# Decay scans whose constant operand lies in PSUM, with a new written-out order, in a fused RWKV and low-rank-mixing kernel

## The chip, the cores and the metric

One NeuronCore of one Trainium2 chip runs the whole kernel in one launch. The metric is the device time of one execution in microseconds (us); lower is better. Before the change it is 448.16 us, the median of 3 runs (447.41 to 448.6).

## What is computed

Two layers follow each other. The first is a linear attention with a decay per channel: batch 4, 8 heads, 768 time steps, 48 channels per head, all in float32.

```python
for t in range(S):
    cur = np.einsum('bhd,bhe->bhde', u[None] * kt, vt)
    y[:, :, t] = np.einsum('bhd,bhde->bhe', rt, state + cur)
    state = wt[:, :, :, None] * state + np.einsum('bhd,bhe->bhde', kt, vt)
```

Its output, with the heads side by side as 384 channels, is x for the second layer: a mix over time of rank 32 (U, V) and an FFN with a hidden width of 1536.

```python
h = x.transpose(0, 2, 1) @ U @ V
u = x + h.transpose(0, 2, 1)
return u + np.maximum(u @ w_ch1, 0.0) @ w_ch2
```

## The kernel before, in words

**The attention** is cut into 24 chunks (4 batches of 6) of 128 time steps; `chunk(g)` (L347) makes the steps of one. The channels of two heads lie on the 128 partitions, four such pairs side by side in the free dimension. The decay w of a chunk comes as four segments of SEG = 129 columns, one zero and then 128 decays, and one column more at the end (L34, L359, L1166). Two scans on VectorE run along these columns, `state = w * state + constant`. Step F (`scan_f`, L385) goes from the end to the start; its constant is `resets`, with a 1 at each segment's border (L187 to L189), so it gives the product of all decays from a time to the chunk's end. Step R (L423) writes the reciprocals of the four totals to the segment starts of `qd` (L218), and step Q (`scan_q`, L398) scans forward with `qd` as its constant. Both constants lie in SBUF. RP (L404) multiplies r by Q, KS (L409) multiplies k by F; either may be on VectorE or on GpSimd. AM (L531) makes the scores on TensorE, CP (L552) masks them, YA and YZ (L615, L640) make the output, DS (L559) the state's increment in the PSUM tile `dS` (L234), and ZA and ZM (L591, L595) add it to the state and let it decay. GpSimd, VectorE or ScalarE have the small products PR, RK, RU, the diagonals SEL and SEL2 and the totals T.

**Turns through TensorE.** For the first 12 chunks, k (KT, L516) and the output (XT, L735) are transposed on TensorE, and for the first 6 the bonus rows (MD, L488) come from there. Each takes the one bank `tr`, which is free again when a copy has taken the result out (KN, XN on ScalarE, DV). Later chunks are transposed in 32 by 32 blocks on VectorE (KD, XD).

**The FFN** works on seven blocks of 384 or 512 times (L29). Mix and block: GA, SELM, HP on TensorE, UADD, UH, UL, then 12 steps UP (L859) and 12 steps DN (L893) of nine matmuls each, in float32r with weights split into a high and a low part. ScalarE or VectorE (HH) and VectorE (HL) take each UP out of its bank. The weights are converted on the chip first (E, C2, C3, ADD, HI, SUB, L287 to L342). The three `ffn` banks serve GA, SELM, HP, UP and DN.

**PSUM** has eight banks: two for the scores, one each for `tr`, `y` and `dS`, three for `ffn`.

**The order** of all 1422 steps is written out by hand in ORDER (L65): of every three characters two give the step's number in base 64, the third says whether it takes its other engine (odd), and how many dummy matmuls `lead` (L202) puts ahead of it (half of it, rounded down). `plan` (L134) only hands out buffer slots along that order. Each engine works off its own steps strictly in it.

```python
        if how % 2:
            s.eng = s.alt
        s.lead = how // 2
```

Of the kernel before, what the change touches and what calls it, by code (L numbers as in the profile page):

```python
# [33 lines left out]
SEG = P + 1  # L34
# [17 lines left out]
def channel_order():  # L52
# [18 lines left out]
    "4p04q17d04f01B00o04a00f07y00b08904b07z05614r11C04V04c00c07h04v04s04W04t04z05D04X10B10d10p05901D00q05E05F10g0"
    "8Z15G17e07-01E04w00s01F05408+00h00z05H00i04x01W04+05I08A14-07l00r14y18107f050M5J61G07g17a07c15101H10t08O05K0"
    "8508-15L00u05O08Q05M00+00j05N00-00v05P07m10k18201I07o05Q05R21008307n15S07q05T05U41107p09i07r05Y08405c07s0120"
    "5V05W05Z07u05a08E05d05e01d05X15b15f18R07v00w08001J01K07w08B17x00x01315m05p00y16208a11L07t15n08C01Y05q05o08T0"
    "5r01f07+01M01P01r08S11N08W11e01g05v01X08D09011Z08b06301a05s01Q06408F01h01b01O11R01y05t01i08r05j01S01c18J01k0"
# [25 lines left out]
    "J10J51Fx0J60J70J80J90Fy0Fz0L20F+0JJ0J21Lx0Lk0J30JD0JV0JE1JF0M40JK0Ln0JL0JW1L50JX0JY0JG0L70JZ0JA0Ja0LC0JB0JH1"
    "JI0JP0JC0JS0JM0JT0L30JQ1JU0Jv1Jb0JN0Jc0JO0JR0L60J-0Lr0Jd0Je0Jz1Lm0J+0Jh0F-0Ji0Jj0M60K00Jf0K11Jk0K20Jn0Lt0Jw1"
    "Lo0Jl0LW0K60M50L+0Jo0L00Lq0Jp0LY0Ly0Lu0K71KC0K80Jq0Lw0L40Jr0KU0KV0KX0Lp0M00KD1Js0M10KW0LX0KI0KE0KY1KJ0KZ0K30"
    "KK0Ka0KR0Jm0Kb1Kc0KL0L-0KS0KM0K41KT0M30K50KO0K90KA0KN0KP1Fv0KB0KF0Kd0L10KG0Lv0KH0Ls0Ke0KQ0M20Kf0Kg0Lz0MA0Kj0"
    "MB0Kh0Kk0Kl0MC0Km0Kp0Ki0Fp0Kn0MD0Kq0Jg0Ko0Kr0Ks0Kt0Ku0"
# [53 lines left out]
def rwkv_moe_kernel(ctx, tc, wT, rkT, vN, vS, rkN, uB, uT, uD, U, V, w1, w2, out):  # L159
# [4 lines left out]
    psT = pool("psT", 1, space=PSUM)  # L164
# [182 lines left out]
    def chunk(g):  # L347
# [133 lines left out]
        if by_pe:  # L481
            btd = Buf("tr")
# [5 lines left out]
            def rows_by_u():  # L488
                tr = st["trd"] = place("tr", [P, NP, P], f"trd_{g}", btd)
# [26 lines left out]
        def turn_k():  # L516
            tr = st["trk"] = place("tr", [P, NP, P], f"trk_{g}", btr)
# [51 lines left out]
        if on:  # L569
# [653 lines left out]
```

## Time and profile before

| What | Value |
|---|---|
| median of 3 runs | 448.16 us (447.41 to 448.6) |
| the profiled execution's own time | 448.02 us |
| its span, first to last instruction | 446.3 us |
| TensorE busy | 426.4 us, 96% |
| VectorE busy | 362.7 us, 81% |
| ScalarE busy | 189.7 us, 42% |
| GpSimd busy | 104.0 us, 23% |
| mean granted TensorE clock | 0.98 |

The profile names the engines PE (TensorE), PEld (its weight loads), DVE (VectorE), ACT (ScalarE), POOL (GpSimd) and SP (the queue that issues DMAs). A line such as "L400 DVE TENSOR_TENSOR_SCAN Q<-w,qd" is an instruction of line 400 on VectorE that writes Q from w and qd. Busy time of an engine is the union of its instructions; an instruction's duration reaches some hundredths of a microsecond into the next one.

### The profile page before, as it was taken

Reading aid. Unit: us, or ns where it says so; the run is one execution under the profiler, and the core shown is the slowest. Engines: PE = TensorE matmul, PEld = TensorE weight load, DVE = VectorE, ACT = ScalarE, POOL = GpSimd, SP = SyncE. Lnnn points to the kernel's source line nnn. Section 1 sums busy time; section 2 is a strip of 40 time slices with the busy share of each in tenths; the row PEclk is TensorE's granted clock in tenths of the full one; section 3 lists DMA queues with packets and bytes.
Section 4 is the critical chain, followed back from the end, with each engine's and each line's share of the span. In section 5 each row is a group of like instructions: output and inputs, shape, how many; then the busy total and the mean of one; then the engine's idle time right before and its main releaser. Section 6 shows DMA issues by size and latency. Waiting matters only on the chain.

```text
span 446.3 us, 9868 instructions
## 1 busy us (share of the span) xinstructions
PE 426.4 (96%) x3906; PEld 366.1 (82%) x3906; DVE 362.7 (81%) x750; ACT 189.7 (42%) x533; POOL 104.0 (23%) x123
## 2 busy tenths in 40 slices
PE   6996999999999999999999999999999999999993
PEld 4785759999999898788868788887767889999993
DVE  8999999999899999999999999999995116524610
ACT  5697988776476332565023323013634002112300
POOL 1112232432257555332225101420000100100000
PEclk9996799999999999999999999999999999999998
DMA  8966836244654635331307030174212130133020
GB/s 298 337 232 225 271 124 220 87 153 151 223 171 164 220 106 181 107 115 37 107 32 241 3 93 0 46 225 164 74 66 77 36 122 21 59 127 110 1 78 24
DMA packets 23911, 57.22 MB, mean 128 GB/s; under 512 B 2864, under 2 KB 7856, under 8 KB 23856
## 3 DMA queue, kind: packets, MB, share of 16 engines
q1 hardware_dynamic: 23856, 56.50, 38.0%
q8 instruction: 32, 0.52, 0.5%
q14 instruction: 23, 0.19, 0.1%
HBM read 51.77 MB, written 4.72 MB: 127 GB/s over the span
## 4 chain that ended last, share of the span: by engine, by line
PE 40%; DVE 16%; issue 1%; ACT 1%; DVEq 0%
PE f L899 20%; PE f L865 16%; DVE xn L720 5%; DVE kn L685 2%; DVE hid L876 2%; DVE xn L718 1%; DVE A L555 1%; DVE F L387 1%; PE aps L542 1%; DVE Q L400 1%; PE hp L816 1%; DVE xT L917 1%; PE y L622 1%; DVE Z L593 0%; PE y L632 0%
## 5 line engine op out<-in xcount | busy, mean ns | idle before, releaser
L865 PE MATMUL f<-u,w1h 128*128 128x384 f32 (+1 forms) x504 | 147.9, 364 | 1.0 <-DVE hid L876 1.0
L899 PE MATMUL f<-hid,w2h 128*128 128x384 f32 (+1 forms) x504 | 148.3, 364 | 0.0
L865 PEld LDWEIGHTS f<-u,w1h 128*128 128x128 f32 x504 | 92.9, 188 | 12.6 <-DVE hid L876 2.5
L899 PEld LDWEIGHTS f<-hid,w2h 128*128 128x128 f32 x504 | 92.9, 188 | 10.0 <-issue 1.3
L865 PE MATMUL f<-u,w1l 128*128 128x384 f32 (+1 forms) x252 | 90.7, 360 | 0.0
L899 PE MATMUL f<-hid,w2l 128*128 128x384 f32 (+1 forms) x252 | 90.7, 360 | 0.0
L870 ACT ACTIVATE hid<-f 128x384 fp32r<-128x384 f32 (+1 forms) x65 | 34.6, 538 | 106.6 <-PE f L865 104.0
L876 DVE SCALAR_TENSOR_TENSOR hid<-f,hid 128x384 fp32r<-128x384 f32 (+1 forms) x84 | 50.2, 606 | 13.4 <-ACT hid L870 12.5
L454 ACT ACTIVATE A<-ident,dv 128x128 f32<-128x128 f32 x148 | 46.6, 391 | 11.7 <-DVE dv L440 3.9
L899 PEld LDWEIGHTS f<-hid,w2l 128*128 128x128 f32 x252 | 47.4, 188 | 4.7
L865 PEld LDWEIGHTS f<-u,w1l 128*128 128x128 f32 x252 | 47.4, 188 | 4.1
L685 DVE STREAM_TRANSPOSE kn<-rk 32x128 f32<-32x128 f32 x160 | 48.3, 302 | 2.4
L917 DVE TENSOR_TENSOR xT<-f,xT 128x384 f32<-128x384 f32 (+1 forms) x21 | 12.8, 613 | 37.6 <-PE f L899 37.2
L322 POOL TENSOR_TENSOR cva_w<-cva_w,raw_w 128x384 int32<-128x384 int32 x24 | 26.2, 1100 | 70.1 <-DVE cva_w L315 51.9
L832 POOL TENSOR_TENSOR u<-xT,u 128x512 fp32r<-128x512 f32 (+1 forms) x11 | 13.5, 1236 | 92.0 <-DVE u L828 85.1
L387 DVE TENSOR_TENSOR_SCAN F<-w,resets 128x517 f32<-128x517 f32 x24 | 30.6, 1275 | 0.4 <-DMA w<-in_wT 0.2
L720 DVE STREAM_TRANSPOSE xn<-xT 32x192 f32<-32x192 f32 x80 | 29.6, 370 | 1.3 <-ACT xT L666 0.2
L400 DVE TENSOR_TENSOR_SCAN Q<-w,qd 128x516 f32<-128x516 f32 x24 | 29.3, 1223 | 0.1
L407 POOL TENSOR_TENSOR rk<-rk,Q 128x512 f32<-128x512 f32 x12 | 16.4, 1365 | 45.0 <-DVE Q L400 42.3
L461 POOL TENSOR_SCALAR_AFFINE_SELECT A<-dv 128x128 f32<-128x128 f32 (+1 forms) x33 | 11.5, 382 | 58.1 <-PE f L865 23.3
L602 ACT ACTIVATE Z<-Z,tots 128x96 f32<-128x96 f32 x60 | 17.5, 364 | 10.3 <-DVE Z L593 10.2
L1088 ACT ACTIVATE junk<-raw_w 128x384 uint8<-128x384 f32 x24 | 13.1, 544 | 19.7 <-DMA raw_w<-in_w 19.5
(123 smaller groups left out, 570.8 us busy)
## 6 DMA issues: line engine op xcount, KB each, us to landing
raw_w<-in_w SPq DMA_DIRECT2D x48, 384.0 KB, 3.9
rk<-in_rkT SPq DMA_DIRECT2D x24, 512.0 KB, 4.3
kr<-in_rkN SPq DMA_DIRECT2D x18, 384.0 KB, 4.5
w<-in_wT SPq DMA_DIRECT2D x24, 258.5 KB, 2.8
v<-in_vS SPq DMA_DIRECT2D x24, 224.0 KB, 3.9
out_dram<-xT SPq DMA_DIRECT2D x12, 192.0 KB, 2.6
out_dram<-xT SPq DMA_DIRECT2D x9, 256.0 KB, 2.5
raw_V<-in_V SPq DMA_DIRECT2D x8, 96.0 KB, 3.4
```

The lines of the kernel that those rows point to most:

```text
L322: lambda: nc.gpsimd.tensor_tensor(out=d["to"].bitcast(I32), in0=d["a"].bitcast(I32), in1=d["e"], op=ALU.add),
L387: nc.vector.tensor_tensor_scan(out=F[:, ::-1], data0=st["w"][:, ::-1], data1=resets[:, ::-1], initial=1.0, op0=ALU.mult, op1=ALU.add)
L400: nc.vector.tensor_tensor_scan(out=st["Q"], data0=st["w"][:, 0:n], data1=qd, initial=0.0, op0=ALU.mult, op1=ALU.add)
L454: nc.scalar.activation(to, one, AF.Copy, scale=dv[:, NP * i + j : NP * i + j + 1])
L602: nc.scalar.activation(st["Z"][:, j], src[:, j], AF.Copy, scale=nxt[:, j : j + 1])
L685: nc.vector.transpose(a, b)
L720: nc.vector.transpose(to[q, :, :, r], src[r, :, :, q])
L865: nc.tensor.matmul(ps, wt[:, f, ct, :], u[ct][:, z], start=(m == 0), stop=(m == 8))
L870: nc.scalar.activation(h[:, 0], d["ps", f], AF.Relu)
L876: nc.vector.scalar_tensor_tensor(out=h[:, 1], in0=d["ps", f], scalar=0.0, in1=h[:, 0].bitcast(F32), op0=ALU.max, op1=ALU.subtract)
L899: nc.tensor.matmul(d["o", ct], wt[:, 4 * ct + part, f - 3 * part, :], hid[f][:, z], start=(part == 0 and m == 0), stop=(part == 3 and m == 8),
L917: nc.vector.tensor_tensor(out=o, in0=d["o", ct], in1=o, op=ALU.add)
```

## The change

The decay segments become SEG = 130 columns: a zero, 128 decays, a zero. One array `qd` now serves both scans: reciprocals at the segment starts, a constant 1 in each segment's last column, zero elsewhere. `resets` is gone. `qd` is 520 columns at the front of a PSUM tile `state` of two banks, and `dS` is the last 384 columns of the same tile. So 512 columns of `qd` fill the first bank, and its last 8 columns share the second bank with `dS`. Both scans read columns of either bank; R writes columns 0, 130, 260 and 390, all in the first. The bank `tr` is gone; MD, KT and XT take one of the three `ffn` banks. ORDER is new.

```diff
-SEG = P + 1
+SEG = P + 2
...
-    psT = pool("psT", 1, space=PSUM)
...
-    resets = const.tile([P, NP * SEG + 1], F32, name="resets")
-    nc.vector.memset(resets, 0.0)
-    nc.vector.memset(resets[:, 0 : NP * SEG + 1 : SEG], 1.0)
+    blank = const.tile([P, 2 * P], F32, name="blank")
+    nc.vector.memset(blank, 0.0)
...
-    busy = resets.bitcast(BF16)[:, 0:512]
+    busy = blank.bitcast(BF16)
...
-    qd = const.tile([P, NP * SEG], F32, name="qd")
+    state = psS.tile([P, 2 * NP * P], F32, name="state")
+    qd, dS = state[:, 0 : NP * SEG], state[:, -NP * ZW :].rearrange("p (j n) -> p j n", n=ZW)
     nc.vector.memset(qd, 0.0)
+    nc.vector.memset(qd[:, SEG - 1 : NP * SEG : SEG], 1.0)
...
-                out=F[:, ::-1], data0=st["w"][:, ::-1], data1=resets[:, ::-1], initial=1.0, op0=ALU.mult, op1=ALU.add
+                out=F[:, :0:-1], data0=st["w"][:, :0:-1], data1=qd[:, :0:-1], initial=1.0, op0=ALU.mult, op1=ALU.add
...
+            r = slice(0, n - 2)
             nc.vector.tensor_tensor_scan(
-                out=st["Q"], data0=st["w"][:, 0:n], data1=qd, initial=0.0, op0=ALU.mult, op1=ALU.add
+                out=st["Q"][:, r], data0=st["w"][:, r], data1=qd[:, r], initial=0.0, op0=ALU.mult, op1=ALU.add
...
-            btd = Buf("tr")
+            btd = Buf("ffn")
...
-                btr = Buf("tr")
+                btr = Buf("ffn")
```

What the new ORDER says, decoded by the rule above (steps by engine, before and after):

| Step | VectorE | GpSimd | ScalarE |
|---|---|---|---|
| RP | 12, 6 | 12, 18 | |
| KS | 14, 8 | 10, 16 | |
| PR | 6, 4 | 0, 2 | |
| RK and RU | 16, 10 | 20, 26 | |
| SUB | 26, 18 | 0, 8 | |
| UL | 10, 12 | 11, 9 | |
| HH | 19, 14 | | 65, 70 |
| SEL and SEL2 | | 11, 16 | 37, 32 |

T, DV, ZM, HI and UH change by one to four steps each. Up to the first UP (UP 0.2 in both), TensorE has the same 51 steps. VectorE has 108 steps there before and 95 after: without 6 RP, 3 KS, 2 PR, 2 RK, 2 SUB, 1 RED and 1 C2, with 2 DV, 1 ZM and 1 R more. GpSimd has 6 RP, 3 KS, 2 PR, 2 RK, 1 RU and 1 SUB more there; ScalarE one each of SEL, SEL2, ZM and T and 2 DV fewer, and one E more. Dummy matmuls: 20 before, all ahead of the first UP; 7 after, five ahead of YA 6 and two ahead of XT 1.0. On the DMA queue the load of the decays of chunk 2 has 2313 KB issued ahead of it where it had 3465 KB; the load of LKR 8 (384 KB) is now one of those ahead of it.

Of the 20 steps DS, 6 stand ahead of the first UP and 14 behind it in the new order. The VectorE step that stands last ahead of a DS is a scan at four of them: DS 0 (Q 3), DS 1 (Q 4), DS 3 (F 7) and DS 15 (F 18).

## Rows read from the trace of the kernel before

**Rows 1.** The page: busy time per engine, and the granted clock in 40 slices.
```profile
PE 426.4 (96%) x3906; PEld 366.1 (82%) x3906; DVE 362.7 (81%) x750; ACT 189.7 (42%) x533; POOL 104.0 (23%) x123
...
PEclk9996799999999999999999999999999999999998
```

**Rows 2.** Windows: start:end, length; busy us per engine; clock, DMA share, GB/s.
```profile
core 0: us, PE busy (x) PEld busy (x) DVE busy (x) ACT busy (x) POOL busy (x), PEclk, DMA share, GB/s
0.00:68.30 68.30, 59.44 (x706) 44.81 (x707) 64.78 (x112) 53.00 (x158) 16.05 (x23) 0.90 0.72 244
68.30:300.00 231.70, 230.73 (x2279) 199.57 (x2278) 223.29 (x471) 102.94 (x282) 82.28 (x95) 1.00 0.39 127
300.00:340.00 40.00, 36.93 (x387) 27.29 (x386) 36.53 (x88) 17.38 (x48) 1.37 (x1) 1.00 0.33 110
340.00:439.40 99.40, 99.27 (x540) 94.39 (x538) 37.55 (x81) 16.36 (x46) 4.27 (x4) 1.00 0.20 66
```

**Rows 3.** Timeline around the first UP, and the last output: start us, us, instruction.
```profile
64.34 0.80 PE L816 MATMUL hp<-Vst,gs 96*128 96x384 f32 x3
...
65.55 1.47 DVE L821 TENSOR_TENSOR xT<-hp,xT 128x384 f32<-128x384 f32 x3
...
66.94 1.48 DVE L832 TENSOR_TENSOR u<-xT,u 128x384 fp32r<-128x384 f32 x3
...
68.31 0.42 PE L865 MATMUL f<-u,w1h 128*128 128x384 f32 x1
...
439.38 0.56 DVE L917 TENSOR_TENSOR xT<-f,xT 128x384 f32<-128x384 f32 x1 [5.69 <-PE f L899]
```

**Rows 4.** Groups on VectorE, shapes apart: count | busy us, mean ns | idle before.
```profile
L387 DVE TENSOR_TENSOR_SCAN F<-w,resets 128x517 f32<-128x517 f32 x24 | 30.6, 1275 | 0.4 <-DMA w<-in_wT 0.2
L400 DVE TENSOR_TENSOR_SCAN Q<-w,qd 128x516 f32<-128x516 f32 x24 | 29.3, 1223 | 0.1
...
L593 DVE TENSOR_TENSOR Z<-dS,Z 128x384 f32<-128x384 f32 x16 | 8.7, 546 | 0.4 <-issue 0.2
...
L407 DVE TENSOR_TENSOR rk<-rk,Q 128x512 f32<-128x512 f32 x12 | 8.2, 680 | 0.0
...
L433 DVE TENSOR_TENSOR kr<-kr 128x384 f32<-128x384 f32 x9 | 4.9, 552 | 0.0
```

**Rows 5.** Timeline of VectorE, a scan and what follows it.
```profile
5.57 1.22 DVE L400 TENSOR_TENSOR_SCAN Q<-w,qd 128x516 f32<-128x516 f32 x1
6.72 0.67 DVE L412 TENSOR_TENSOR rk<-rk,F 128x512 f32<-128x512 f32 x1
7.30 1.23 DVE L387 TENSOR_TENSOR_SCAN F<-w,resets 128x517 f32<-128x517 f32 x1
```

**Rows 6.** Groups on ScalarE, shapes apart.
```profile
L454 ACT ACTIVATE A<-ident,dv 128x128 f32<-128x128 f32 x148 | 46.6, 391 | 11.7 <-DVE dv L440 3.9 <-PE f L899 3.1 <-PE y L632 2.9
...
L602 ACT ACTIVATE Z<-Z,tots 128x96 f32<-128x96 f32 x60 | 17.5, 364 | 10.3 <-DVE Z L593 10.2
```

**Rows 7.** Groups on GpSimd, shapes apart.
```profile
L407 POOL TENSOR_TENSOR rk<-rk,Q 128x512 f32<-128x512 f32 x12 | 16.4, 1365 | 45.0 <-DVE Q L400 42.3 <-DVE tots L396 2.7
...
L433 POOL TENSOR_TENSOR kr<-kr 128x384 f32<-128x384 f32 x9 | 9.2, 1025 | 1.9 <-DMA kr<-in_rkN 1.9
```

**Rows 8.** Timeline of VectorE and GpSimd where both read SBUF.
```profile
125.22 1.21 DVE L387 TENSOR_TENSOR_SCAN F<-w,resets 128x517 f32<-128x517 f32 x1
125.44 1.99 POOL L407 TENSOR_TENSOR rk<-rk,Q 128x512 f32<-128x512 f32 x1 [7.04 <-DVE Q L400]
...
127.38 1.20 POOL L412 TENSOR_TENSOR rk<-rk,F 128x512 f32<-128x512 f32 x1
```

**Rows 9.** What TensorE waited for: total us, times, longest.
```profile
PE trk L520 <- ACT xn L743: 1.0, 1, 1.0
...
PE trd L200 <- ACT kn L529: 0.7, 1, 0.7
```

**Rows 10.** Timeline of TensorE in the first 30 us.
```profile
10.00 2.08 PE L550 MATMUL aps<-rk 48*128 48x128 f32 x16
...
15.68 0.88 PE L564 MATMUL dS<-v,kn 128*48 128x48 f32 x16
...
26.27 1.16 PE L550 MATMUL aps<-rk 48*128 48x128 f32 x16
```

More of the change, by code (lines that the diff above doesn't have):

```diff
@@ L71 @@
[L71 to L75, printed above, removed]
@@ L101 @@
[L101 to L105, printed above, removed]
+    "2x03602y03003202z00J03713M03503N03303P03803908Y00L03R03n00K00M03W13413U03A13C03B13V03S03E03113X03D03F03o03Q1"
@@ new lines @@
+    "3T13q02-03s00N03w03x04C03Y13t04D03d03Z11403a10004F00103v03y04M04d03e00Q01603z04H03b03O01503u04000O00204K14e0"
+    "1707i03+14I05304L03G03c03r13I00P14g00C01804n14i00S03J04J11904N00300T03H14j05204203f00R04G10U03-10D00V05C14k1"
+    "4o00504O15504m00408605703p03i03g04h14304P14103j00E04Q13k05B01A17Z07Y04l15D00600X05A15E08713h14p00W10700F00Y0"
+    "4407h00804E00l00m04T07b04708Z00G00H02+04507j08+05F15804f04804U00904R00Z03K00I14q10a00n08-17y05600o08a0590490"
+    "1B07d04r10A03L00p07-04614S07z00e04s04u05G14Y04Z00q00B04V04A00b04a07e04v04W00z05400c04b04t00d11D04z08P08504X1"
@@ new lines @@
+    "1C05H04c00g01E00s00r17k18108r04+05I08014B04w04x00+03l04-07l05007f14y05J08818410-00h01F01G03m01H15K00f07g08O0"
+    "8207m10u05O05L01007a07+05M05105N00v07n17o05P00i01I05Q00t07q05R07r01100j07uA5S05T07p00w05U08R05V05Y05Z07v00x0"
+    "5W05c05d08315a07w45X15e01201d07x05b15f11J01e08T07s00y18E01P01W05m01X08905n01310k08A15s01f01Y05p05t01g01h08B1"
+    "1k01K05o08b06201L01Z05u01i01M02A01N01a01r08F05q15j05r06305k05g06407c11j11l01O15h05l09001m01R08C01n01S05i01Q0"
+    "1o08U05-09101b01T02H08q01c18V08D08W11t05y01U16508X09G01V16002B08g07t11p02C01s05z06601u08J01v02I01y08c18K02D0"
@@ new lines @@
+    "8G05+01q08d08S15v08t08L06701w05w06W02V01z01x02E06101+02305x06X06B06802J02K06C06E01-02002106D08H02L08Q0690220"
+    "2408h06A09P08e02508f08y12602F02j08v06F08I12702O02M16G06a08z08w09406H09209J06b08i02G18l02809k02918m08x1960931"
+    "8j06Y02N12P09j09502l08u12Q02m06K02X08n06Z02R02c06L06I06e02S02k02W02n06M02T06f02U19i08o08M06c18k16d16N02Y02Z0"
+    "8s09702q09K12e08p02a06g02b12d09809L06O06h12f09B09C09H09D09l08N06x02g09E09M0BL02h09F09902r07A02i09s09r06Q02s0"
+    "Bc02o09O16y06J09m19t09u09n06R09N07B06z0BM19Q07C06l02t0BB02u06m09o07D0Bb06n02p09R19Y07E09S09A1BE07707F02v06S0"
@@ new lines @@
+    "BC07806o02w0BK09v0Bk0BF19T07909U06T09V06p19q09W09p19I06q06U0Ch06i0BJ09Z0BN09w19X06V06u06r0BR06v06w0DB09a0BS0"
+    "9d06P0BG09x1BH09e0BI16j06s0Bl09y0C509b07106t0BO06+06k0Be09c19z07409f09+0C70720Bj09-0BV0BP0Bg0Bh07306-0C807G0"
+    "700Bm0C60BT0BD09g0Bi1BQ17H0750760Bn0Ci0CY0A007I0BW0Bo0A10Cj0Bf1CA0A20CE07J09h0CX0A30Br0CB0BZ0DC0Bp1A40BU0CC1"
+    "CD1Ca0CF0Ck0A507K0Bv0D10Cg0Ga0C91Bs0BX07M0D20A60Bt0A70Bu0Bq0D407N0A807O0Ba0D51A90CG1Bd0DD0Cb1AD0BY07P0AE0CL0"
+    "Cc0AA07S07T0Bw0CM0Dd0DE0AH0AB0H407U0CN0Cf0Cd07V0CH0Cl1DU0DT0AF0AI0Bx0AJ0D60AC0B+0AG07W0DF1B-0Cm0AK0Gb0C007Q0"
@@ new lines @@
+    "H50CI0Cn0CP0Ag0CO0Ce1AX0Co0Ah0Am0Ai0AL0GA0CJ1DW0CZ0An0D707X0CK0CQ0De0DA0DY0By0C10Cr07R0AY0Ao0AM0Bz1CR0G00CU0"
+    "CV0Df0AU0GB0D81AV0AZ0CS0Dc0DZ0Aa0Ab07L0CT1AN0Cs0AR0C20D90DH0H60AW0Cp0Ac0Ap0Db0CW0DI0Ad0Cq0DJ0DG0GQ0Da1Ae0Cw0"
+    "H70G10D30Dg0Af0G90DX0G30Cx0AS0Aq0Ct0Gc0DL0Ar0AT0Dh1As0GR0Cy0Cu0AO0G50DM0Aj0DK0Ha0Cv1Cz0AP0DN0Dj0DQ0DV0GC1Di1"
+    "G60AQ0Ak0DR0H80Al0DO0At1Dk0Au0DP1DS0Av0C+0Aw0GZ0C30G71GT0Ax0Dl0Dm0C-0Hb0Gd0D00Ay0HR0Gw0C40A-0B00Dn0Ky0Do0H91"
+    "B10Dp0G20Dq0Dr0Kz0G80B20Ds0Dt0GD0GK0Du0GY0I40GE0GF0GV0B30Dv0B50Gg0Dw0Gx0Az0B40Dx0Gh0Dy0Dz0GL0E00B60E10D+1E40"
@@ new lines @@
+    "B70E50D-0GG0E20E60B80E71E31Ge1EZ0A+0GH0E80GI0IW0B90H30K+0EK0Hc1E90GU1GW0EA0Ea1HQ0G40I50EL0Eb0GS0EQ0GJ0GX0ER0"
+    "EE0HZ0EF0ES0EB0Gi0EM0BA0IX0EG0EN0HT0Hd0Gz0Ef0GO0G-0Gk0I61HY0IY0Gj0EC0GM0Eg0Eh0LZ0HU1E+0HS0EO0ED0EW0H00E-0Gf0"
+    "H20GN1GP0EX0EP0HV0I70H10Gl0Hw0HA0G+0Ec0EH0EI0EY0Gm0Gp0Gq0HW0Hg0Ed0HE0HX1Ee0IM0Hh0HB0EJ0Ei0Hz0ET0Gr0F20He1EU0"
+    "F30EV0Ll0Hx0Ej0Gs0I20HC0Gy0Ek0F60IP0El0H-0Eo0HF0Em0HD0Hf1Ep0Hk0IZ0Hi0Gn0Gt0F01HG0Go1HJ0HH0HK0H+1IN0Eq0Er0IA0"
+    "Eu0LN0I00Hj0HL0HM0Gu0Lb0En0HI1Ev0IR0F70I11L50Ew0Hm0F40LB0IB0Hl0Lm0IV0Ia1I80Es0Hp0F50LT0Hn0LC0F80I90LV0Hq0IQ1"
@@ new lines @@
+    "IO0IS0HN0IE0Ex0F90L60F10FP0FV0IC0LU0Et0FW0Gv0LK0Ey0ID0FQ0Ib0FS0FX0Fb0Ho0FR0LQ0IU0LO0Ln0LL0HO0FA0FT0Ez0Hy0LH0"
+    "IF0Fc0Hr0Lf0FU0IT1IG0Kv0Fd0LD0Hs0IJ0IK0Ic0Ht0IH0FM0FD0L70FB1Hu0FC0LM0I30Id0IL0Hv0FJ0HP0FN0II1Lh0FO0FE1Ie0If0"
+    "FK0FF0Il0LJ0Ig0L80FL0FG0Ih0L20FH0Ii0FI0Ij0Fe0Ik0Fk0Im0LP0LI0La0In0L90Io0Lg0Fl0Ip0Iq0Ff0Ir0LS0Fg0Is0Iv0Iw0Jt0"
+    "Iz0Ju0I+0Jx0Jy0FY0FZ1It1Fa0Li0LA0Fh0Ix0Iu1Fi1Fj0Fm0Lj0Iy1Fn0I-0J01Kx0Fq0J10LR0Lx0Lk0Fo0J40Fr0Fs0J50J20J30J60"
+    "Ft0Fu0Fw0J70J80J90JG0Fx0Fy0Jv1JH0Fz0JA0L40JI0K-0F+0Jw0JJ0JK0Lr0JL0JB0JD0JM0Lc0JE1JF0JN0JV0JC0JO0JW0JP0L30JQ1"
@@ L106 @@
+    "JX0JY0Lo0JS0JR0JZ1Ja0Jb0Jz1JT0JU0Jc0J-0Kw0Jd0Le0Je0Jh0M10K00Jf0Ji0M20Jj0Jk0Jn0L+0Jl0Jo0J+1K10K21K60Jm0KX0LE0"
+    "Lz0LW0Fp0KY1Jp0Fv0KZ0F-0L10Lp0Ld0M40Ls0KF0Jq0Lt0KG0KH0M70K70Lu0KU0Jr0K90KV0Jg0Lq0M90K80KW0KI0KA0KC0M50KB0KD0"
+    "KO0KP0KJ1Ly0KE0M00M30KQ0KR0LY0LX0LG0Lv0KK0KL0K30KS0L-0KM1KT0Ka0LF0K40M60M80K50Kd0Kb0Lw0KN0Ke0L00MA0Kf0MB0Kc0"
+    "Kg0Kj0MC0Kk0Kl0Km0Kp0Kn0Js0MD0Kq0Kh0Kr0Ko0Ks0Ki0Kt0Ku0"
 )
@@ L172, in rwkv_moe_kernel @@
     stage = pool("stage", 1)
-    slots = dict(big=BIG_BUFS, w=W_BUFS, v=2, F=2, Q=1, dv=2, kn=2, Z=2, tr=1, y=1, ffn=3, xT=3, xn=NCH // 2, cva=CVA_BUFS, g4=1, gs=2)
-    homes = dict(big=big, tr=psT, y=psY, ffn=psF, xT=xtp, cva=stage)
+    slots = dict(big=BIG_BUFS, w=W_BUFS, v=2, F=2, Q=1, dv=2, kn=2, Z=2, y=1, ffn=3, xT=3, xn=NCH // 2, cva=CVA_BUFS, g4=1, gs=2)
+    homes = dict(big=big, y=psY, ffn=psF, xT=xtp, cva=stage)
     turns = dict.fromkeys(slots, 0)
@@ L488, in rows_by_u @@
             def rows_by_u():
-                tr = st["trd"] = place("tr", [P, NP, P], f"trd_{g}", btd)
+                tr = st["trd"] = place("ffn", [P, NP, P], f"trd_{g}", btd)
                 lead(tr)
@@ L516, in turn_k @@
         def turn_k():
-            tr = st["trk"] = place("tr", [P, NP, P], f"trk_{g}", btr)
+            tr = st["trk"] = place("ffn", [P, NP, P], f"trk_{g}", btr)
             lead(tr)
@@ L732, in turn @@
             return
-        btr = Buf("tr")
+        btr = Buf("ffn")
         def go():
-            tr = d["tr"] = place("tr", [P, NP, P], f"trx_{b}_{c}", btr)
+            tr = d["tr"] = place("ffn", [P, NP, P], f"trx_{b}_{c}", btr)
             lead(tr)
@@ L948, in recurrence @@
                 st, vt = (full("xT", f"{n}_{j}") for n in ("st", "vt"))
-                nc.sync.dma_start(chunks(wt), wb[:, :, j * SEG + 1 : (j + 1) * SEG])
+                nc.sync.dma_start(chunks(wt), wb[:, :, j * SEG + 1 : j * SEG + 1 + P])
                 nc.sync.dma_start(chunks(rt), rb[:, 0, j])
@@ L955, in recurrence @@
                     nc.sync.dma_start(vn, vb4[:, c, j])
-                    tr = place("tr", [P, NP, P], f"trv_{j}_{c}")
+                    tr = place("ffn", [P, NP, P], f"trv_{j}_{c}")
                     nc.tensor.transpose(tr[0:VW, 0, :], vn, ident)
@@ L1164, in chunked @@
         return t
[L1166 to L1167 removed]
+    wT = np.zeros((B, NCH, P, NP * SEG), f32)
+    wT.reshape(B, NCH, P, NP, SEG)[..., 1 : 1 + P] = chunked(w, 1.0)
     rkT = np.stack([chunked(r, 0.0), chunked(k, 0.0)], axis=3)
```

48 lines of the change are left out of this document (8 added, 40 removed).

## The prediction, made before the changed kernel ran

> **What bounds the kernel now.** I read the page first, then the windows, then the timeline at the border that the windows show. The page gives TensorE 426.4 us of a 446.3 us span at a mean clock of 0.98 and VectorE 362.7 [rows 1]; such a mean hides that there are two stages. The windows separate them [rows 2]. Up to 68.3 us VectorE is busy for 64.78 us of 68.3; TensorE is idle for 8.9 us and runs partly at the lower clock (slices 4 and 5 of the clock line read 6 and 7 [rows 1]). From the first UP at 68.31 us [rows 3] TensorE is full: it idles 231.70 - 230.73 = 0.97 us up to 300 us, 3.07 us from 300 to 340, 0.13 us up to the end of the last DN at 439.4. Behind that come one addition and the last output DMA, together 7 us of the span. So two numbers set the end: **when the first UP can start**, and **how long TensorE then needs**, 371.1 us of which 4.2 us are idle. The change leaves the 51 TensorE steps ahead of the first UP and all those behind it as they are, so a microsecond that the first UP comes earlier is one at the end, as long as TensorE stays fed.
>
> The first UP hangs on HP, three UADD, UH and UL [rows 3], and these on the first six chunks, whose steps stand in VectorE's queue. I count a VectorE step not by its duration but by the start of the next: Q starts at 5.57 and the next at 6.72, 1.15 us for a duration of 1.22; KS takes 0.58 of 0.67 [rows 5]. So 0.07 to 0.09 us come off each duration.
>
> **The change, part by part.**
>
> *Steps that leave VectorE before the first UP.* 6 RP, 3 KS and 2 PR at 0.60 (0.68 less 0.08 [rows 4]) are 6.6 us. 2 RK, 2 SUB and 1 RED at 0.47 (0.55 less 0.08 [rows 4]) are 2.35 us; one ZM comes, priced as the addition Z<-dS,Z at 0.47 [rows 4]; one C2 goes and 2 DV and 1 R come, all short, which I let cancel. That is 6.6 + 2.35 - 0.47 = 8.5 us off a queue that was busy 64.78 us: the upper bound of what the first stage can gain. ScalarE loses one SEL and one SEL2 (four ACTIVATEs of 0.39 each, 1.56 a step) and one ZM (four of 0.36, 1.46 us) [rows 6], and gets an E, which I bound by one ACTIVATE of 0.39 to 1.0: some 3.6 us off 53.00 busy [rows 2]. If ScalarE becomes the limit, 3.6 us is the gain. GpSimd gets 11 long steps at 1.20 (its clean duration at 127.38 [rows 8]) and 4 at 1.03 [rows 7], 17.3 us on top of 16.05 [rows 2], half of the stage; it is no bound, but RP and KS there are 0.5 us longer than on VectorE, in the chain of every early chunk. I take **6.0 us**, the middle of 3.6 and 8.5, since VectorE was the fuller engine but the chunk's own chain grows.
>
> *The scans with a PSUM operand.* No scan in this trace reads PSUM. The nearest rows are an addition with one operand in PSUM, 546 ns, and a product of the same size with both in SBUF, 552 ns [rows 4]: equal. I take 0. Bounds: a gain of up to 0.8 us per collision that vanishes, since a GpSimd product that started 0.2 us into a scan took 1.99 us instead of 1.20 [rows 8]; a loss of 48 scans by the 0.08 us by which one could lose its overlap with the next step, 3.8 us of VectorE time, of which 17 scans or 1.4 us lie before the first UP. [...]
>
> *The shared bank.* The last 8 columns of `qd` lie in the bank of `dS`, so a DS on TensorE and a scan on VectorE that the order puts ahead of it can't overlap any more: **DS waits for the scan, and behind DS waits all of TensorE's queue**; a scan that stands behind a DS waits for it, and behind it VectorE's. DS takes 0.88 us at the lower clock [rows 10]. Six DS fall before the first UP, where TensorE has idle time; three scans stand between such a DS and the ZA that needs it anyway, at most 2.6 us of VectorE's queue, which is why I stay off the upper bound of 8.5. Of the 14 DS behind the first UP one (DS 15) has a scan as VectorE's last step ahead of it. Bounds: nothing, or 14 whole scans, 16 us. I take one scan, **+1.1 us**, by the order.
>
> *Turns in the `ffn` banks.* Before the first UP only GA, SELM and HP use these, so three banks replace one: the two waits for a copy of another turn, 1.0 and 0.7 us [rows 9], can go, and the 13 dummy matmuls less are also TensorE time; both are covered by VectorE, so 0. Behind it 9 KT and XT take one of three banks for about a microsecond each while UP and DN run. Bounds 0 and 9 us; I take 0, since a bank is held by one UP only until HH and HL have read it.
>
> *Behind the first UP* VectorE has some 8 us less work (4 RU or RK, 3 KS, 6 SUB, 5 HH, each 0.47 to 0.60, less 2 UL). It was full there, 223.29 of 231.70 us and 36.53 of 40.00 [rows 2], and the 3.07 us of TensorE's idle time from 300 to 340 us lie in its last stretch. I take **2.0 us** of these off; bounds 0 and 4.2.
>
> *Loads and initial fills*: the decays of chunk 2 have less ahead of them on the queue; LKR 8 comes early but behind what the first two chunks need. 0, hidden by the chunk before; if not, 384 KB at the 244 GB/s of this stage [rows 2], 1.6 us once.
>
> **Sum.** -6.0 - 2.0 + 1.1 = -6.9 us against the profiled execution's 448.02 us (446.3 us span and 1.7 around it), which is 0.14 below the median of the runs. That gives **441.1 us**.
>
> **The rivals.**
>
> *The first stage is held by something else.* [...] Then -2.0 + 1.1 remain: 447.1 us (445.5 to 449). [...] Chance 0.13.
>
> *GpSimd isn't freed* (the change does not do what it says): products on it still stretch from 1.20 towards 1.99 us [rows 8] beside VectorE's other two-operand steps. Fifteen such steps before the first UP, half of them hit by 0.8 us, cost 6 us on GpSimd, of which I put half on chunks' chains: 444.1 us. Chance 0.08. [...]
>
> *The scans take longer* by the lost overlap: 1.4 us before the first UP, 442.5 us. Chance 0.05.
>
> *Slower: the shared bank.* TensorE, full behind the first UP, does not keep the order's times; each of 14 DS meets a scan that VectorE has just begun or not reached. At half a scan each it is 14 x 0.57 = 8.0 us, which takes back all of the gain; from a mean wait of 0.67 us on, the kernel is slower by 0.3% or more, and at a whole scan each, 16 us, it is 456 us. I put this case at 452 us. For it: the scans are 48 of VectorE's largest steps and TensorE has no idle time to hide it. Against: from chunk 12 on DS waits for VectorE's KD anyway. [...] Chance 0.17.
>
> **How the numbers follow.** The forecast itself has 0.57, with 436.5 (8.5 and 3.0 us gained, nothing lost) to 445 as its own range. A difference under 0.3%, 1.3 us, is about what a measurement of this kernel can't tell from none. Faster by more: 0.57 + 0.08 + 0.05, about 0.70. Within: the held first stage, 0.13. Slower: 0.17. The range 437 to 449 us leaves out most of the slower case (0.15) and some 0.03 at the fast end.
>
> **What would show it.** Right: the first UP at 62 us (60 to 65); VectorE's busy time down by about 16 us, GpSimd's up by about 30; F and Q at 1.2 to 1.25 us; GpSimd's RP at 1.2 us beside a scan; less than 2 us of idle time of TensorE before its DS; idle from 300 to 340 us at about 1 us. Wrong: a first UP at 67 or later with matmuls of twice their length ahead of it; a row in TensorE's waits in which DS waits for a scan, many times; scans that grow past 1.3 us.

## The result, and the profile after

The kernel after takes 451.52 us (median of 20 runs, 447.82 to 455.97), the kernel before beside it 447.68 us: a ratio of 1.0075, 95% interval 1.0046 to 1.0104. It is slower, by 3.8 us between these medians and by 0.75%, or 3.4 us, by the ratio; 441.1 us was forecast, and the range ended at 449. Two of the 20 runs, at 454.87 and 455.97 us, lie in a slower state, and the ratios, here and below, leave such runs out.

The profiled execution took 450.96 us, its span is 449.3 us. Most line numbers are one higher than before. The page, busy time per engine and granted clock:

```profile
PE 424.3 (94%) x3893; PEld 366.5 (82%) x3893; DVE 346.9 (77%) x721; ACT 182.9 (41%) x513; POOL 131.9 (29%) x156
...
PEclk9999999999999999978999999999999999999998
```

Against [rows 1]: VectorE has lost 15.8 us of work and GpSimd has gained 27.9, as forecast. The saving is there; it just didn't reach the end. The windows show where it went (columns as in [rows 2]):

```profile
0.00:68.30 68.30, 56.13 (x701) 44.17 (x702) 61.98 (x110) 51.10 (x150) 34.82 (x40) 1.00 0.81 270
68.30:300.00 231.70, 228.61 (x2260) 197.18 (x2260) 210.01 (x443) 98.62 (x272) 89.71 (x107) 0.99 0.38 120
300.00:340.00 40.00, 38.19 (x398) 29.42 (x392) 37.24 (x88) 14.74 (x41) 6.38 (x10) 1.00 0.33 103
```

From 68.3 to 300 us TensorE, which before idled 0.97 us there, now idles 231.70 - 228.61 = 3.09 us. From 300 to 340 it idles 1.81 us instead of 3.07. TensorE's waits (total us, times, longest) name the new thing:

```profile
PE state L565 <- DVE Q L401: 3.1, 2, 2.7
PE state L565 <- DVE F L387: 2.6, 1, 2.6
PE state L565 <- DVE state L424: 2.4, 2, 1.6
```

Line 565 is DS, the state sum; its tile is now called `state`. Before, no row had DS waiting for a scan. Now it waits 8.1 us in all: for Q, for F, and, not expected, for R (line 424), which writes only columns of the first bank. The timeline says at which DS (start us, us, instruction, in brackets the idle time before it):

```profile
21.42 0.88 PE L565 MATMUL state<-v,kn 128*48 128x48 f32 x16 [2.68 <-DVE Q L401]
...
51.90 0.56 PE L565 MATMUL state<-v,kn 128*48 128x48 f32 x16 [0.77 <-DVE state L424]
...
65.01 0.18 DVE L424 RECIPROCAL state<-F 128x4 f32<-128x4 f32 x1
...
65.24 0.56 PE L565 MATMUL state<-v,kn 128*48 128x48 f32 x16 [1.62 <-DVE state L424]
...
66.83 0.44 PE L866 MATMUL f<-u,w1h 128*128 128x384 f32 x1
```

These are DS 0 (behind Q 3), DS 4 (behind R 7) and DS 6 (behind R 8). The profile infers these releasers from semaphore events: they show an order that the program keeps, and what the bank itself would do no run here shows. None of the 20 DS of this trace runs beside a scan or an R; in the trace of before six of 20 do (DS at 205.13 us, for 0.56 us, inside a scan F from 205.10 to 206.33). DS 6 starts 0.05 us after R ends, and the first UP stands two steps of TensorE behind it: at 66.83 us, only 1.48 us earlier than before [rows 3], where 62 was expected. The fourth is DS 15:

```profile
196.73 1.23 DVE L387 TENSOR_TENSOR_SCAN F<-w,state 128x519 f32<-128x519 f32 x1
...
198.01 0.89 PE L565 MATMUL state<-v,kn 128*48 128x48 f32 x16 [2.60 <-DVE F L387]
...
201.33 0.63 PE L866 MATMUL f<-u,w1h 128*128 128x512 f32 x1
...
204.87 0.39 PE L866 MATMUL f<-u,w1h 128*128 128x512 f32 x1
...
209.30 1.23 DVE L401 TENSOR_TENSOR_SCAN Q<-w,state 128x518 f32<-128x518 f32 x1 [4.11 <-issue]
```

TensorE stands still for 2.60 us because F 18 is at work. Then the same matmul takes 0.63 us instead of 0.39, and in windows of 0.5 us the granted clock reads 0.50 from 198 to 204 us, and 1.00 up to 197.5 and from 204.5 on. And since TensorE comes late, scan Q 18 waits 4.11 us: it stands behind DS 16 (208.63 us). The pause comes back as idle time on VectorE. Windows of the stretch:

```profile
195.00:200.00 5.00, 2.40 (x60) 2.04 (x56) 4.75 (x10) 3.12 (x11) 0.00 (x0) 0.77 0.37 105
200.00:205.00 5.00, 5.00 (x24) 3.92 (x17) 4.37 (x10) 0.80 (x4) 0.00 (x0) 0.55 0.01 3
205.00:210.00 5.00, 5.00 (x69) 3.94 (x71) 0.89 (x2) 1.50 (x5) 0.00 (x0) 1.00 0.15 40
```

In the clock column, 0.23 and 0.45 of 5 us each are missing: at most 3.4 us of TensorE's work, since part of the first stretch is the pause. The account closes: the last addition starts at 441.64 us instead of 439.38 [rows 3], 2.26 later. The first UP came 1.48 earlier, so TensorE took 3.74 us longer from there. Of these 1.0 us is more idle time (5.17 us from the first UP to the last addition, 4.15 before) and 2.7 us more busy time (369.64 against 366.92) for the same matmuls, which is what the lower clock can account for.

The scans themselves cost nothing more. Groups on VectorE and GpSimd (busy us, mean ns):

```profile
L387 DVE TENSOR_TENSOR_SCAN F<-w,state 128x519 f32<-128x519 f32 x24 | 29.5, 1227 | 3.6 <-DMA w<-in_wT 1.2 <-ACT w1h L331 0.7 <-ACT tots L394 0.6
L401 DVE TENSOR_TENSOR_SCAN Q<-w,state 128x518 f32<-128x518 f32 x24 | 29.4, 1226 | 6.8 <-issue 4.1 <-PE state L565 1.6 <-ACT Z L603 0.8
...
L408 POOL TENSOR_TENSOR rk<-rk,Q 128x512 f32<-128x512 f32 x18 | 22.1, 1225 | 27.9 <-DVE Q L401 26.4 <-PE trx L740 1.5
```

1.227 and 1.226 us stand against 1.275 and 1.223 [rows 4], and GpSimd's RP needs 1.225 instead of 1.365 us [rows 7].

### The profile page after: what moved, and what is told of

Its sections match the earlier page's. It is cut to its first block, busy times and chain, and to the rows that moved or that the text cites. A ratio compares the mean times of both kernels' runs of the same rounds, so it can differ in the third digit from the quotient of the medians.

```text
span 449.3 us, 9846 instructions
## 1 busy us (share of the span) xinstructions
PE 424.3 (94%) x3893; PEld 366.5 (82%) x3893; DVE 346.9 (77%) x721; ACT 182.9 (41%) x513; POOL 131.9 (29%) x156
## 4 chain that ended last, share of the span: by engine, by line
PE 75%; DVE 15%; ACT 2%; issue 1%; DMA 1%; DVEq 0%
PE f L900 31%; PE f L866 28%; PE aps L543 2%; PE state L565 2%; DVE hid L877 2%; PE y L623 2%; DVE kn L686 2%; DVE xn L721 2%; PE aps L551 2%; PE y L633 2%; PE y L646 1%; DVE xn L719 1%; PE ga L763 1%; DVE A L556 1%; DVE Q L401 1%
## 5 line engine op out<-in xcount | busy, mean ns | idle before, releaser
L866 PEld LDWEIGHTS f<-u,w1h 128*128 128x128 f32 x504 | 93.9, 190 | 11.7 <-DVE hid L877 0.9
L871 ACT ACTIVATE hid<-f 128x384 fp32r<-128x384 f32 (+1 forms) x70 | 36.9, 536 | 126.6 <-PE f L866 118.1
L455 ACT ACTIVATE A<-ident,dv 128x128 f32<-128x128 f32 x128 | 40.4, 392 | 3.7 <-DVE dv L500 1.4
L401 DVE TENSOR_TENSOR_SCAN Q<-w,state 128x518 f32<-128x518 f32 x24 | 29.4, 1226 | 6.8 <-issue 4.1
L833 POOL TENSOR_TENSOR u<-xT,u 128x512 fp32r<-128x512 f32 (+1 forms) x9 | 11.3, 1264 | 71.5 <-DVE u L829 65.5
L387 DVE TENSOR_TENSOR_SCAN F<-w,state 128x519 f32<-128x519 f32 x24 | 29.5, 1227 | 3.6 <-DMA w<-in_wT 1.2
L408 POOL TENSOR_TENSOR rk<-rk,Q 128x512 f32<-128x512 f32 x18 | 22.1, 1225 | 27.9 <-DVE Q L401 26.4
L413 POOL TENSOR_TENSOR rk<-rk,F 128x512 f32<-128x512 f32 x16 | 19.4, 1211 | 32.1 <-DVE F L387 18.0
L827 ACT ACTIVATE u<-xT 128x384 fp32r<-128x384 f32 (+1 forms) x15 | 8.5, 571 | 35.8 <-PE f L900 22.0
```

The source lines that it names most:

```text
L387: nc.vector.tensor_tensor_scan(out=F[:, :0:-1], data0=st["w"][:, :0:-1], data1=qd[:, :0:-1], initial=1.0, op0=ALU.mult, op1=ALU.add)
L401: nc.vector.tensor_tensor_scan(out=st["Q"][:, r], data0=st["w"][:, r], data1=qd[:, r], initial=0.0, op0=ALU.mult, op1=ALU.add)
L455: nc.scalar.activation(to, one, AF.Copy, scale=dv[:, NP * i + j : NP * i + j + 1])
L866: nc.tensor.matmul(ps, wt[:, f, ct, :], u[ct][:, z], start=(m == 0), stop=(m == 8))
L871: nc.scalar.activation(h[:, 0], d["ps", f], AF.Relu)
```

## The experiments

Two theories stood at the start. **A**: the tie between DS and the scans (one tile, a shared bank) eats the saving. **B**: the new order itself is no better. All ratios are against runs of the kernel before on the same chip, with 95% intervals. The kernels ran on several chips, so where two of them are compared below, the difference of their ratios stands beside that of their medians.

### The tie taken away by another place for the constant

The constant back to SBUF, DS alone in its bank, all else as after:

```diff
-    state = psS.tile([P, 2 * NP * P], F32, name="state")
-    qd, dS = state[:, 0 : NP * SEG], state[:, -NP * ZW :].rearrange("p (j n) -> p j n", n=ZW)
+    qd = const.tile([P, NP * SEG], F32, name="qd")
+    dS = psS.tile([P, NP, ZW], F32, name="dS")
```

> The changed kernel, with its new order and its turns in the ffn banks, but the shared scan constant lies in SBUF again and dS has a bank of its own, so nothing ties TensorE's DS to VectorE's scans. Theory A (the time is lost by the tie: DS waits for a scan or a reciprocal, 8.1 us of TensorE's idle time in the changed kernel): those waits go, under 1.5 us is left, the first UP comes at 62 to 65 us instead of 66.8, the clock does not fall near 200 us, and the time is 441 to 445 us. Theory B (the new order itself is no better, its chains through GpSimd are longer): other waits take their place, the first UP stays at 66 us or later, 447 to 451 us. GpSimd's RP should stretch again beside scans, from a mean of 1.225 us towards 1.3.

Measured: 457.66 us, 1.0206 (1.0153 to 1.0258). Both theories missed. No DS waits for a scan any more, but the other price is larger: GpSimd's busy time is 165.6 us instead of 131.9 and VectorE's 366.0 instead of 346.9. Where a scan with two SBUF operands and a product of GpSimd overlap, both can take longer, here 2.23 and 2.19 us against means of 1.23 and 1.27 in after (timeline):

```profile
16.66 2.19 POOL L487 TENSOR_TENSOR kr<-rk 128x512 f32<-128x512 f32 x1
17.71 2.23 DVE L387 TENSOR_TENSOR_SCAN F<-w,qd 128x519 f32<-128x519 f32 x1
```

F takes 1.468 us in the mean, Q 1.416, and the first UP comes at 75.37 us. Without the PSUM operand the two engines have 52.8 us more of busy time in this order (33.7 and 19.1), and the kernel is 6.1 us longer (457.66 - 451.52; 5.9 by the ratios) although the pauses for the tie are gone.

Two kernels kept most of the constant in PSUM, in a bank of its own (columns 0 to 389, the rest in SBUF; then 0 to 511, the rest in SBUF), each scan cut in two at that column:

```diff
+    qd = psA.tile([P, 4 * P], F32, name="qd")
+    qt = const.tile([P, SEG], F32, name="qt")
...
+                out=F[:, : m - 1 : -1], data0=st["w"][:, : m - 1 : -1], data1=qt[:, ::-1],
...
+                out=F[:, m - 1 : 0 : -1], data0=st["w"][:, m - 1 : 0 : -1], data1=qd[:, m - 1 : 0 : -1],
```

> New order, turns through TensorE in the banks of the channel mix, constant of the scans still in PSUM for three of the four pairs of heads, but in a bank of its own (390 columns); the fourth pair's 130 columns in SBUF; the state sums alone in their bank. Each scan and each reciprocal becomes two instructions, about 72 more small ones on VectorE (estimate 5 us of its busy time, most of it beside other work). Theory A (the tie between state sums and scans through the shared bank costs the time): no state sum waits for a scan or a reciprocal, first UP at 62 to 65.5 us, 442 to 447 us. Theory B (the new order itself is no better): 449 to 453 us, state-sum waits gone all the same. A third possibility (scans of three pairs with a SBUF remainder collide with GpSimd as in the kernel with the whole constant in SBUF): GpSimd busy over 145 us and 452 to 458 us.

> New order; the scans' constant lies in a PSUM bank of its own for columns 0 to 511 and in SBUF for the last 8, the state sums alone in their bank. Each scan is cut into 512 columns and a rest of up to 8, so that hardly any of it reads two SBUF operands (the split by pairs of heads still had scans of 130 SBUF columns that took up to 1.3 us beside GpSimd). Theory A (the tie between scans and state sums is what costs): no state sum waits for a scan; VectorE's busy time under 356 us (the split by pairs had 361.4); 442 to 447 us. Theory B (the new order itself is no better): state-sum waits gone, 448.5 to 452 us.

Measured: 450.29 us, 1.0063 (1.0031 to 1.0094), and 458.72 us, 1.0239 (1.0211 to 1.0266); both outside what A expected; the first lies in the range of B, the second beyond both. DS waits for no scan in either, but VectorE's busy time is 361.4 us in the first, where 72 small instructions were to cost 5 us. The groups of the second kernel show why:

```profile
L395 DVE TENSOR_TENSOR_SCAN F<-w,F,qd 128x511 f32<-128x511 f32 x24 | 30.7, 1277 | 0.8
L413 DVE TENSOR_TENSOR_SCAN Q<-w,qd 128x512 f32<-128x512 f32 x24 | 29.1, 1211 | 0.3
L391 DVE TENSOR_TENSOR_SCAN F<-w,qt 128x8 f32<-128x8 f32 x24 | 12.0, 499 | 0.4 <-DMA w<-in_wT 0.2
```

Eight columns with two SBUF operands take 155 ns at the least and 499 in the mean; beside this product of GpSimd they take 1.15 us (timeline):

```profile
22.63 1.36 POOL L420 TENSOR_TENSOR rk<-rk,Q 128x512 f32<-128x512 f32 x1 [0.40 <-DVE Q L413]
22.87 1.15 DVE L391 TENSOR_TENSOR_SCAN F<-w,qt 128x8 f32<-128x8 f32 x1
```

Both end at about 24.0 us. The first UP of the two kernels comes at 69.17 and 70.11 us, later than the 66.83 of after. TensorE is no busier up to there (54.7 and 55.2 us, in after 54.7), though the clock column reads 0.78 in both for the first 68.3 us and 1.00 in after: the time was lost in waits. What the cut costs hides what the tie cost; these runs don't decide between A and B.

### The tie turned round everywhere

In the written order, twelve scans or reciprocals stand close ahead of nine DS, so that DS waits for them (DS 0, 1, 3, 4, 6, 8, 13, 15 and 18; at some of them one to three other steps lie between, which DS could pass). All twelve turned: DS first, the scan waits for it; each engine's own order is that of after.

```diff
-Q 3, ..., DS 0
+DS 0, ..., Q 3
...
-F 18, YZ 15, HH 2.2, HH 2.10, DS 15
+YZ 15, HH 2.2, HH 2.10, DS 15, F 18
```

> The changed kernel with the constant in PSUM and the shared bank; every engine works off the same steps in the same order, only some DS are written ahead of the neighbouring scan or reciprocal of VectorE instead of behind it, so that where the two collide VectorE waits for TensorE and not the other way round. Theory A: TensorE's waits for scans and reciprocals fall from 8.1 us to under 3, VectorE's waits for DS grow from 2.2 to some 4 us, the first UP comes at 63 to 65.5 us, time 443 to 447 us. Theory B: no gain, 449 to 452 us.

Measured: 456.87 us, 1.0186 (1.0134 to 1.0238), slower than either expected. No DS waits for a scan or a reciprocal any more, but VectorE waits for DS (total, times, longest):

```profile
DVE Q L401 <- PE state L565: 7.3, 4, 3.2
DVE F L387 <- PE state L565: 5.8, 2, 5.3
...
DVE state L424 <- PE state L565: 2.8, 2, 1.4
```

That is 15.9 us, where theory A had some 4, and later TensorE waits 5.0 us for VectorE in one piece (HP at 265 us). The tie costs in both directions: a scan put behind a DS waits for everything that TensorE has ahead of it, up to 5.3 us here.

### The tie turned round where TensorE waited

Only the four DS that the profile shows waiting 0.77 us or more: DS 0 ahead of Q 3, DS 6 ahead of R 8, R 7 behind DS 4, F 18 behind DS 15. TensorE's order stays as it was; on VectorE only CP 5 now goes ahead of R 7.

```diff
-Q 3, LRK 5, GUARD 3, DS 0
+DS 0, ..., Q 3, LRK 5, GUARD 3
...
-R 7, LRK 9, YZ 4, CP 5, T 7, XN 0.2, DS 4
+LRK 9, YZ 4, CP 5, T 7, XN 0.2, DS 4, R 7
...
-UL 0.0, ..., R 8, DS 6
+DS 6, UL 0.0, ..., R 8
...
-F 18, YZ 15, HH 2.2, HH 2.10, DS 15
+YZ 15, HH 2.2, HH 2.10, DS 15, F 18
```

> The kernel after, with the order turned round at four places only: the four state sums that waited for VectorE (2.7, 0.8, 1.6 and 2.6 us) are written ahead of the scan or reciprocal that held them, which now waits for the sum instead; TensorE's order is unchanged, VectorE's only in one pair. Theory A (those pauses, and the lower clock that followed the one at 198 us, are what the change lost): first UP by 65 us, clock at 0.99 or more, 443 to 448 us, and less spread from run to run than the 447.8 to 456 us of the kernel after. Theory B (the pauses are slack; the order itself is no better): 449 to 452 us.

Measured: 442.9 us (442.28 to 443.89), 0.9908 (0.9892 to 0.9924): faster than both kernels, 8.6 us below after by the medians, 7.5 by the ratios. B falls: the new order is better once these four pairs are turned. A holds, with two of its signs missed: the time is 0.1 us under its range, and the mean clock is 0.97 to 0.98, not 0.99. Windows of the profiled execution, and the first UP:

```profile
0.00:68.30 68.30, 59.61 (x718) 47.97 (x719) 63.90 (x114) 53.79 (x158) 35.56 (x41) 0.90 0.80 270
68.30:300.00 231.70, 231.09 (x2362) 198.88 (x2361) 215.97 (x458) 97.01 (x268) 95.79 (x115) 1.00 0.39 126
```

```profile
62.30 0.56 PE L565 MATMUL state<-v,kn 128*48 128x48 f32 x16
...
63.89 0.44 PE L866 MATMUL f<-u,w1h 128*128 128x384 f32 x1
```

The first UP is 2.94 us earlier than in after, and behind it TensorE idles 0.61 us up to 300 us where after had 3.09. The clock did not decide this: up to the first UP TensorE is busy for 55.20 us here and 54.66 in after, and its idle time is 8.69 us against 12.17. The clock column, 0.90 here and 1.00 in after, would mislead. In after it reads 1.00 from 20 to 40 us, yet the 16 score matmuls of a step AM take 2.08 us in the first half of that stretch and 1.16 in the second:

```profile
25.90 2.08 PE L551 MATMUL aps<-rk 48*128 48x128 f32 x16
...
35.20 1.16 PE L551 MATMUL aps<-rk 48*128 48x128 f32 x16
```

Then the halves of it. The three pairs ahead of the first UP alone, and the fourth (F 18 and DS 15) alone:

> Of the four places that the kernel measured at 442.9 us turned round, only the three before the first UP (state sums that waited 2.7, 0.8 and 1.6 us). Theory A1 (the first stage carries the loss): first UP at about 64 us, the pause of some 2.6 us near 195 us stays, and 444 to 447 us. Theory A2 (the pause at 198 us with the lower clock behind it carries the loss): 447 to 451 us.

> Only the fourth place turned round: scan F of chunk 18 now stands behind the state sum that waited 2.6 us for it at 198 us. Theory A1 (the first stage carries the loss): 447.5 to 450.5 us, first UP still near 66.8 us. Theory A2 (the pause at 198 us and the clock behind it carry it): 444 to 447.5 us and no run above 451 us.

Measured: 447.3 us, 0.9992 (0.9963 to 1.002), and 446.77 us, 0.9978 (0.9953 to 1.0002). Against after they win 4.2 and 4.7 us by the medians, 8.9 together, and both at once 8.6; by the ratios it is 3.7 and 4.3, together 8.0, and both at once 7.5. Within what the intervals tell, the parts add up. Both times lie in the ranges of A2 (the first is 0.3 us above that of A1, the second 0.7 below), but A2's account, in which the pause at 198 us carries the loss, leaves no room for what the first three pairs win, and A1's none for the fourth: neither half carries it all. The three pairs bring the first UP to 65.11 us, not to 64; in the three traces without them it stands at 66.55 to 67.67 us, in the three with them at 63.68 to 65.11. The first kernel still has its pause of 2.60 us and the lower clock behind it (windows):

```profile
190.00:195.00 5.00, 3.71 (x65) 2.78 (x63) 4.81 (x15) 2.77 (x7) 0.00 (x0) 1.00 0.09 7
195.00:200.00 5.00, 3.70 (x54) 3.11 (x55) 4.91 (x11) 2.32 (x8) 0.00 (x0) 0.77 0.29 102
```

The second has none: TensorE works 4.94 of the 5 us from 195 to 200 us at clock 1.00. Its first UP is at 67.67 us, so it won nothing ahead of that; from there to the last addition it takes 370.05 us, where after takes 374.81. So one scan, moved behind four steps of other engines, is worth 4.8 us in the traces: 2.5 us less busy time (367.14 against 369.64), which the lower clock can account for (at most 3.4 us in after), and 2.3 us less idle time.

A fifth pair, for the 3.06 us that DS 1 waited for Q 4 in the kernel of 442.9 us:

```diff
-Q 4, LW 5, AM 2, DS 1
+LW 5, AM 2, DS 1, Q 4
```

> The four places of the kernel measured at 442.9 us, and a fifth: scan Q of chunk 4 behind the state sum that still waited 3.1 us for it at 25.9 us there. If each pause on TensorE in the first stage reaches the first UP: 440 to 442 us and first UP at 61 to 62.5 us. If VectorE's queue sets the first UP once the four are gone: 442 to 444 us, first UP still at about 64 us.

Measured: 444.44 us, 0.9925 (0.9895 to 0.9954), first UP at 63.68 us: no further gain; the time is 0.4 us above even the second of the two ranges. The wait went, but not the time; other waits took its place (2.7 us for a mask, 1.5 us for a decayed state on ScalarE). So this pause of 3.1 us in the first stage was slack.

### The old order

The old order with the constant in SBUF, DS in its own bank, and four turning banks; so before, but for the shared turns, the 130th column and one constant for both scans:

> Order and engine choice of the kernel before; constant of the scans in SBUF, state sums in a bank of their own, four turning banks shared by the channel mix and the turns through TensorE; segments of 130 columns as after. It differs from the kernel before in the shared turning banks, the 130th column and the single constant for both scans. Theories A and B both: 446.5 to 449 us (layout and turns cost nothing). Rival (turns in the banks of the channel mix cost): over 451 us.

Measured: 447.08 us, 0.9988 (0.9958 to 1.0019). With four banks, those three parts of the change cost nothing that shows.

The old order under the layout of after (three turning banks; KT 7, XT 1.1, UP 0.0, KT 8, XT 1.2, UP 1.1, UP 1.7 and UP 1.8 had to move later for that), then the same with the constant split by columns as above:

> The data layout of the changed kernel (constant in PSUM, shared bank, turns in the ffn banks) under the order of the kernel before; eight TensorE steps are put a few places later, since three banks can't hold what four did. Theory A: the old order knows nothing of the tie, so some of 20 DS meet a scan; TensorE's waits in DS are 2 to 8 us and the time is 449 to 455 us. Theory B (the layout is harmless, the new order is at fault): 446 to 448.5 us, DS waits under 1.5 us.

> The repaired old order with three turning banks (that of the kernel measured at 467.8 us), but with the scans' constant split as in the kernel above, so that the state sums share no bank with it. Theory A: the 7.9 us of state-sum waits for scans and reciprocals go and 455 to 461 us come out. Rival (the fourth turning bank and the repair of the order were what cost there): 464 to 468 us.

Measured: 467.81 us, 1.0444 (1.0392 to 1.0495), and 458.49 us, 1.0237 (1.019 to 1.0284). An order that knows nothing of the tie pays for it: 7.9 us of DS waits in its trace, and 9.3 us come back without it, as A expected of the second run, though the cut scans cost VectorE something there too. The first run was dearer than either theory had it. What is left, 458.5 against 447.1 us, is the fourth bank, the eight moved steps and the cut scans; their shares were not separated.

### Why R is tied

R writes columns 0, 130, 260 and 390, all in the first bank, but as a stretch that ends at 520. The same with a stretch that ends at 392, on the kernel of 446.77 us:

```diff
-nc.vector.reciprocal(qd[:, 0:n:SEG], st["F"][:, 1:n:SEG])
+nc.vector.reciprocal(qd[:, 0 : n - P : SEG], st["F"][:, 1 : n - P : SEG])
```

> The kernel measured at 446.8 us (scan F 18 behind its state sum), with one slice written shorter: the reciprocal addresses its four columns 0, 130, 260 and 390 as a stretch of 392 columns instead of 520, so that the stretch itself ends in the first bank. If the reciprocal was tied to the state sums because its stretch reached into their bank: no state sum waits for a reciprocal (2.4 us there), first UP at 64.5 to 66 us, 443.5 to 445.5 us. If it is tied in another way (through the scan before it in the queue, or through the whole tile): the waits of 0.8 and 1.6 us stay, first UP at 67 to 68 us, 446 to 447.5 us.

Measured: 446.96 us, 0.9992 (0.9961 to 1.0024). DS still waits 2.4 us for R, with pieces of 0.76 and 1.62 us. So the stretch was not the reason. Nor is it the scan ahead of R in the queue: DS 6 starts 0.05 us after R itself ends in after, and 0.06 here. That the tie goes by the whole tile fits, but no run shows it.

## Why the prediction was wrong, step by step

**The shared bank, +1.1 us: this step failed.** The mechanism was priced as the slower rival (452 us, 0.17), and it is what happened, at 451.5 us; but not by that rival's working, so that the two times lie close together is luck. It spread half a scan over each of 14 DS behind the first UP. In the trace one such DS pays (DS 15, the very one that the prediction counted) and three ahead of the first UP. That a DS and a scan keep out of each other's way the trace shows (none of the 20 DS overlaps one in after); that the bank is the reason, as the prediction has it, no run shows. The step was off in three ways.
- For DS 15 it took one scan, 1.1 us. The pause was 2.60 us, since TensorE was ready at 195.4 us, while VectorE came to the scan at 196.73 only, behind reductions, an HL and a copy; and the lower clock came on top. Undoing it was worth 4.7 us (4.3 by the ratios).
- Ahead of the first UP it charged VectorE's queue only, "where TensorE has idle time". TensorE paused 2.68 + 0.77 + 1.62 us there; undoing that was worth 4.2 us (3.7 by the ratios). DS 6 stood two steps ahead of the first UP, so its wait could not be slack.
- It went by the DS that have a scan as VectorE's last step ahead of them. Two of the four pauses were for R. DS 1 and DS 3, which have one, did not wait in after.

**The first stage, -6.0 us: right in kind, hidden by the tie.** After shows -1.48. With the four pairs turned the first UP comes at 63.89 us, 4.42 earlier than before and within the 60 to 65 that were expected. Of the 4.5 us by which after missed this term, 2.9 are the tie by that trace (1.7 by the one with only the first three pairs turned). The other 1.6 us would be a middle taken too high; which engine or chain sets the first UP once the pairs are turned, no run shows.

**Behind the first UP, -2.0 us:** with the pairs turned, the last addition starts at 433.31 us, 369.42 us behind the first UP, against 371.07 before: -1.65 us. The idle time from 300 to 340 us fell to 1.81 us in after and 2.05 there, not to 1.

**Right:** the scans at 1.23 us with a PSUM operand (a difference priced at 0), GpSimd freed, VectorE down by 15.8 and GpSimd up by 27.9 us. **The turns in the channel mix's banks** at 0 held in the old order with four banks; with three it was not tested by itself.

The sum without the term of the shared bank, 441.1 - 1.1 = 440.0 us, is 3 us from the 442.9 of the kernel in which four pairs are turned. The sign hung on that term: with four pairs turned, the change is faster, as forecast.

## What to carry to other kernels

Before two engines' operands go into one PSUM tile, write down for each pair which of the two runs first and what stands in both queues ahead of it; a tie costs the later engine's whole lag, not the length of the instruction (2.60 us at DS 15, for a scan of 1.23). In a written order, turn only the pairs at which the profile shows a wait: four of them were worth 8.6 us here (7.5 by the ratios), all twelve cost 5. Price a pause of TensorE in a full stretch with the lower clock that can follow it: behind the 2.60 us it was 0.55 over 5 us in after, 0.89 in the kernel with the first three pairs turned.

## What the runs showed of the hardware that was not expected

**Even a scan of eight columns, with two SBUF operands, can last until a GpSimd instruction beside it ends.** It took 0.16 us at the least and 1.19 at the most, 0.50 in the mean. Ten of the 24 took more than 0.5 us; two of these, begun 0.24 and 0.50 us behind a product of GpSimd at 22.63 and 28.48 us, end 0.03 and 0.02 us after it. The 130-column rest of the other cut took 0.74 in the mean.

**A pause of 2.6 us was followed by the lower clock.** The granted clock was 0.77 from 195 to 200 us and 0.55 in the 5 us behind them; in the kernel with the first three pairs turned, which has the same pause, it was 0.77 and 0.89; with the pause gone it stayed at 1.00 there. In the 20 runs of after, five of the six at a mean clock of 0.996 or more took 447.8 to 448.5 us, what before takes, and the five at 0.955 or less 453.0 to 454.4. The mean clock is no measure by itself: with F 18 alone turned, three runs at 0.957 took 446.7 to 448.2 us, no more than the nine others, and the column can read 1.00 over slow matmuls, as shown above.

**A scan whose start value is a column, not a number, was slower:** 1.277 us for 511 columns, against 1.211 for 512 with a number, both with the constant in PSUM. The column had just been written by the scan ahead of it; which of the two cost the 0.07 us was not separated.
